# Reordering the first attention layer's start and the denominator and statistics work of a four-layer transformer kernel

## The chip, the cores and the metric

The kernel runs on one core of a Trainium2 chip. A core has five engines with an instruction queue each: TensorE (PE in the profile, matrix multiplication), VectorE (DVE), ScalarE (ACT), GpSimd (POOL) and SyncE (SP), which here only issues DMA transfers. A queue is worked through in order: an instruction that waits holds back all that stands behind it on its engine. Matmuls accumulate in PSUM, a memory of eight banks per partition; everything else lies in SBUF, 128 partitions wide.

The metric is the device time of one execution, in microseconds (us), as the median of several runs.

## The reference

Four residual layers are applied to x of shape 2048 rows by 576 columns (S = 2048, D = 576), in bfloat16: attention, MLP, attention, MLP, with the same two sets of weights used twice.

```python
def _A_ref(x, wqkv, wo):                       # H = 32 heads of 18
    q, k, v = split_heads(x @ wqkv)
    phi = lambda t: where(t > 0, t + 1, exp(t)) + 1e-6
    pq, pk = phi(q), phi(k)
    kv = einsum("bhsd,bhse->bhde", pk, v)      # sums over all rows
    z = einsum("bhsd->bhd", pk)
    num = einsum("bhqd,bhde->bhqe", pq, kv)
    den = einsum("bhqd,bhd->bhq", pq, z)[..., None] + 1e-6
    return merge_heads(num / den) @ wo

def _B_ref(x, w1, b1, w2, b2):                 # F = 4608
    return gelu(layernorm(x) @ w1 + b1) @ w2 + b2

x = x + _A_ref(layernorm(x), A_wqkv, A_wo)
x = x + _B_ref(layernorm(x), B_w1, B_b1, B_w2, B_b2)
x = x + _A_ref(layernorm(x), A_wqkv, A_wo)
x = x + _B_ref(layernorm(x), B_w1, B_b1, B_w2, B_b2)
```

Attention is linear: `kv` and `z` are sums over the whole sequence, so queries can be finished only after all keys and values have been seen.

## The kernel before

**Units.** Rows go in 16 tiles of 128 (t = 0 to 15); four tiles make a block of 512 rows (c = 0 to 3, j the tile within it). The 576 columns are five groups of heads, g = 0 to 3 with 126 columns (seven heads) and g = 4 with 72 (four heads). The four layers are li = 0 to 3, here called layer 1 to layer 4; layers 1 and 3 are attention (`layer_A`), 2 and 4 the MLP (`LayerB`).

**Layer norm pipe** (`LNPipe`). A row tile that is fed to it moves one stage with every tick: statistics on VectorE (two halves, L293 and L294, aggregate L299, variance plus epsilon `ln_u` in L302 or L304), then GpSimd computes `ln_rstd` (L309) and `ln_nmr` (L313), then the normalized tile goes to one of three `y_ring` buffers (on GpSimd L324, on VectorE L328), then five 128x128 transposes on TensorE write `tp` (L346) and ScalarE copies them to `yT` (L348). In the argument `after` the caller names an instruction behind which the statistics must stand in VectorE's queue; this sets an order only and is no wait.

**Attention, first loop.** For each tile: `k_proj` makes the keys in two halves of 288 columns, five matmuls each (L441), into one of four rotating PSUM banks (`ps_h`). phi is then built in one of two ways. `phi_from_psum`: exp on ScalarE (L381), a second ScalarE pass adding the constant (Identity, L382), then on VectorE a minimum with 1 (L383) and a maximum of the two (L385). `phi_by_dve`: exp on ScalarE (L368), the minimum on VectorE (L369), and one VectorE operation that reads PSUM directly (L371). Before the change the second half goes by `phi_by_dve` in layer 3 only. The buffers for the exponentials (`phi_e`) are three, those for the Identity results two. Then `pre_a1` ticks the pipe (in layer 1 it first feeds tile t + 3, whose statistics stand behind the last phi product), `v_proj` makes the values in two column halves of 252 and 324 (L454, L457), both in the single PSUM tile `v_ps` of two banks; ScalarE copies 504 columns (L459), and the last 72 go by ScalarE for t < 2 (L462) and by VectorE otherwise (L464). `kv_acc` adds the tile before into `kvacc` (L472), and from some t on one query projection `q_proj` is added per tile (L478).

In layer 1, `k_proj(1)` comes directly behind `k_proj(0)`. Tiles 0 and 1 are normalized on VectorE, the others on GpSimd.

**Attention, between the loops.** VectorE masks `kvacc` to the heads' diagonal blocks (`kvT`) and builds `zsel`. `kv_wo(g)` multiplies a group of `kvT` with `wo` and copies the result to `kvwo` (L528 on VectorE for odd g, L530 on ScalarE for even). `den_stage(c)` computes the denominators of block c (L538, L542), their reciprocal (L546, VectorE, one buffer) and `quad_rden` (L548, VectorE), a masked copy that lies ready as a matmul operand. `scale_stage(g, c)` broadcasts it to all columns of a group by one matmul (L554 into `rden_ps`), copies that on ScalarE (L556) and multiplies it into the queries `pq` on VectorE (L557).

**Attention, wo loop.** For each tile, `wo_stage` makes ten matmuls (L565), two halves with g = 0 to 4 in order, so the fifth needs the scaled queries of g = 4, into `wo_ps`, which alternates between two PSUM tiles (accA, accB): tile t's matmuls must wait for the residual sum of tile t - 2 (`residual`, L419, VectorE). The new row tile is stored, and tiles 0 to 3 are fed to the layer norm pipe for the next layer. Behind `wo_stage` come scales of the next block (two, two, one and none for j = 0 to 3), in layer 1 the query projections that are left, `den_stage(c + 2)` once per block, and one tick of the pipe.

**What sets the order.** TensorE's instructions are chained by hand in program order (`pe`), and start-up transfers likewise (`chained`). On the other engines the build orders instructions by estimated readiness, bound by data and by the orders named by hand (`add_manual_dep` with NOSYNC).

Of the kernel before, what the change touches and what calls it, by code (L numbers as in the profile page):

```python
# [8 lines left out]
ALU = mybir.AluOpType  # L9
# [25 lines left out]
def build(tc, A_x, A_wqkv, A_wo, B_w1, B_b1, B_w2, B_b2, out, dbg=None, n_layers=4):  # L35
    nc = tc.nc
    dbg = dbg or {}
    with ExitStack() as ctx:
# [225 lines left out]
        class LNPipe:  # L264
# [3 lines left out]
            def feed(self, xt, t, kind, norm_eng, evac_eng="dve", load_from=None, after=None):  # L268
                self.items.append(dict(stage=(0 if load_from is None else -1), xt=xt, t=t, kind=kind,
                                       norm=norm_eng, evac=evac_eng, load=load_from,  # L270
                                       after=after))
# [4 lines left out]
            def tick(self, transposes=1):  # L276
                land()
                for it in list(self.items):
                    st = it["stage"]
                    if st == 4 and it["evac"] != "dma":  # L280
                        if transposes == 0:
                            continue
                        transposes -= 1
                    if st == -1:
# [5 lines left out]
                    elif st == 0:  # L290
# [4 lines left out]
                        if it["after"] is not None:  # L295
                            for stats in (first, second):
                                tc.add_manual_dep(stats.ins, it["after"], NOSYNC, reason="statistics give way")
# [3 lines left out]
                        if it["kind"] == "A":  # L301
                            nc.vector.tensor_scalar(out=u[:], in0=mv[:, 1:2], scalar1=EPS, scalar2=None, op0=ALU.add)  # L302
                        else:
                            nc.vector.tensor_scalar(out=u[:], in0=mv[:, 1:2], scalar1=1.0 + EPS, scalar2=EPS * EPS,  # L304
                                                    op0=ALU.mult, op1=ALU.add)
                        it["mv"], it["u"] = mv, u
                    elif st == 1:
# [50 lines left out]

        lnp = LNPipe()
# [15 lines left out]
        def phi_from_psum(ps_ap, out_ap, rows, n, turned_cols=False):  # L375
# [6 lines left out]
            nc.scalar.activation(out=a_out, in_=ps_ap, func=ACT.Identity, bias=C1, scale=1.0)  # L382
# [46 lines left out]
        def layer_A(li, next_kind, pre_a1=None):  # L429
# [5 lines left out]
            def k_proj(t):  # L435
                tok = slice(t * P, (t + 1) * P)
                pk = blk.tile([P, D], BF16, name="pk", tag="blk")
                for half in range(2):
# [5 lines left out]
                    phi = phi_by_dve if li > 0 and half == 1 else phi_from_psum  # L444
# [3 lines left out]
            def v_proj(t):  # L448
# [4 lines left out]
                for k in range(KD):  # L453
                    pe(nc.tensor.matmul(vp[:, 0, 0:252], lhsT=yT[:, k, tok], rhs=wqkv_sb[:, k, 2 * D: 2 * D + 252],  # L454
                                     start=(k == 0), stop=(k == KD - 1)))
                for k in range(KD):
                    pe(nc.tensor.matmul(vp[:, 1, 0:324], lhsT=yT[:, k, tok], rhs=wqkv_sb[:, k, 2 * D + 252: 3 * D],  # L457
                                     start=(k == 0), stop=(k == KD - 1)))
                nc.scalar.copy(out=va[:, 0:4, 0:126].rearrange("p (b g) c -> p b g c", b=2),  # L459
                               in_=vp[:, :, 0:252].rearrange("p b (g c) -> p b g c", g=2))  # L460
                if t < 2:
# [24 lines left out]
            for t in range(NT):  # L486
                if t != 1 or li > 0:
                    k_proj(t)
                if t == 0 and li == 0:
                    k_proj(1)  # L490
# [41 lines left out]
            quad_rden = {}  # L532

            def den_stage(c):
# [10 lines left out]
                with nc.allow_low_precision("reciprocal of the denominator in the reference's bfloat16"):  # L545
                    nc.vector.reciprocal(out=rden[:], in_=dp[:, 0:P])  # L546
                quad = blk.tile([P, D], BF16, name="quad_rden", tag="blk")
                nc.vector.tensor_tensor(out=quad[:, 0:CA].rearrange("p (j n) -> p j n", j=4), in0=quad_mask[:],  # L548
                                        in1=rden[:].unsqueeze(1).to_broadcast([P, 4, P]), op=ALU.mult)
# [10 lines left out]
            def wo_stage(t):  # L560
# [8 lines left out]
                if xn is not None and next_kind == "B" and t < TPC:  # L569
                    lnp.feed(xn, t, "B", "pool", "act")  # L570
# [7 lines left out]
            den_stage(0)  # L578
            q_proj(*q_left.pop(0))
            kv_wo(1)  # L580
            den_stage(1)
# [3 lines left out]
            q_proj(*q_left.pop(0))  # L585
            for g in range(3, G):
                scale_stage(g, 0)
            kv_wo(3)
            kv_wo(4)
            q_proj(*q_left.pop(0))  # L590
            for t in range(NT):
# [3 lines left out]
                wo_stage(t)  # L595
                if c + 1 < NCA:
# [153 lines left out]
        def pre_a1_layer0(t):  # L750
            if t + 3 < NT:
                feed0(t + 3, after=dve_last["phi"])
# [79 lines left out]
```

## Time and profile before

| | |
|---|---|
| median of 3 runs | 778.01 us (777.93 to 779.69) |
| profiled execution, its own time | 778.13 us |
| its span, first to last instruction | 776.4 us |
| granted TensorE clock, mean | 1.000 |

Busy time of the engines in stretches of that execution (us):

| stretch | from, to | PE | DVE | ACT | POOL |
|---|---|---|---|---|---|
| layer 1, start | 0 to 18 | 13.64 | 11.34 | 8.70 | 6.44 |
| layer 1, rest of first loop, preparation | 18 to 84 | 65.32 | 49.00 | 54.07 | 32.01 |
| layer 1, half of the wo loop | 84 to 103 | 18.49 | 17.63 | 11.01 | 10.03 |
| rest of it, layer 2 | 103 to 397 | 294.00 | 90.66 | 104.25 | 35.06 |
| layer 3 up to the wo loop | 397 to 465 | 67.31 | 40.36 | 47.87 | 0.55 |
| rest | 482 to 777 | 290.83 | 51.10 | 101.06 | 26.67 |

How such lines are read: a timeline row gives the start in us from the beginning of the span, the length in us, the engine, the line of the kernel, the operation, the tile written and the tiles read, their sizes and the number of equal instructions in a row. In brackets stands how long the engine had been idle before it, and whose end it waited for. PE is TensorE and the length of a run of matmuls includes the pipeline's last result, so the next row can start before the one above has ended; the same holds for the other engines by smaller amounts. The step of an operation is therefore taken from one start to the next.

### The profile page before, as it was taken

The page shows a single profiled execution, that of the slowest core. Times are in us where ns is not written, and L with a number is a line of the kernel's source. Part 1 is how long each engine was busy: PE and PEld are TensorE (multiplying, and loading weights), DVE is VectorE, ACT ScalarE, POOL GpSimd, SP SyncE. Part 2 cuts the span into 40 slices and gives each one's busy share as a digit, 9 for nine tenths or more (in the row PEclk, how much of TensorE's full clock was granted, in tenths as well). Part 3 has the DMA queues.
Part 4 walks back from the last instruction along what each step waited for, and adds up shares of the span by engine and source line. Part 5 has one row for each costly group of instructions (what it writes and reads, how often), then busy time and mean ns, then how long its engine had stood idle before and what let it go on. Part 6 is the DMA issues. An engine that isn't in the chain of part 4 may idle for free.

```text
span 776.4 us, 15770 instructions
## 1 busy us (share of the span) xinstructions
PE 765.1 (99%) x6613; PEld 495.6 (64%) x6613; DVE 276.4 (36%) x711; ACT 335.4 (43%) x738; POOL 119.2 (15%) x185
## 2 busy tenths in 40 slices
PE   7999999999999999999999999999999999999998
PEld 4777664575477457646777766547745764675476
DVE  5786965045113603400355579520140032000000
ACT  4887746403620660164046675561065026304600
POOL 3573312012000301200100004210030011002000
PEclk9999999999999999999999999999999999999999
DMA  8990374106401720230440006730141033011000
GB/s 268 278 296 22 111 242 121 36 31 171 109 16 48 187 61 32 80 75 2 153 100 9 1 2 208 250 81 8 31 128 53 17 124 80 8 32 54 1 11 21
DMA packets 73761, 69.10 MB, mean 89 GB/s; under 512 B 34266, under 2 KB 58330, under 8 KB 73690
## 3 DMA queue, kind: packets, MB, share of 16 engines
q1 hardware_dynamic: 73690, 68.10, 30.2%
q8 instruction: 51, 0.84, 0.5%
q14 instruction: 20, 0.16, 0.1%
HBM read 45.67 MB, written 22.41 MB: 88 GB/s over the span
## 4 chain that ended last, share of the span: by engine, by line
PE 94%; DVE 3%; ACT 1%; issue 1%; POOL 0%; DVEq 0%; ACTq 0%; POOLq 0%
PE m_ps L716 36%; PE h_ps L666 20%; PE hp_ps L666 16%; PE k_ps L441 5%; PE q_ps L478 5%; PE wo_ps L565 4%; PE v_ps L457 3%; PE v_ps L454 2%; PE kvacc L472 1%; PE tp L346 1%; PE warm_ps L176 1%; PE rden_ps L554 1%; ACT rden_bc L556 1%; DVE pq L557 0%; DVE xn L419 0%
## 5 line engine op out<-in xcount | busy, mean ns | idle before, releaser
L716 PE MATMUL m_ps<-w_sb,hT 128*128 128x288 bf16 x2304 | 283.6, 286 | 0.0
L716 PEld LDWEIGHTS <-hT 128*128 128x128 bf16 x2304 | 224.8, 98 | 59.8 <-issue 3.4
L666 PEld LDWEIGHTS <-w_sb 64*128 64x128 bf16 x2304 | 124.6, 94 | 136.4 <-issue 1.9
L666 PE MATMUL hp_ps<-yT,w_sb 64*128 64x512 bf16 x1152 | 178.0, 376 | 0.0
L666 PE MATMUL h_ps<-yT,w_sb 64*128 64x512 bf16 x1152 | 148.0, 376 | 0.0
L671 ACT COPY relay_sb<-relay_sb 128x1 f32<-128x1 f32 x144 | 28.5, 198 | 264.7 <-PE h_ps L666 222.2
L309 POOL TENSOR_TENSOR ln_rstd<-ln_u,neg_half 128x1 f32<-128x1 f32 x64 | 36.4, 571 | 483.3 <-DVE ln_u L302 253.0
L662 ACT ACTIVATE hT<-h_ps,b1T 128x512 bf16<-128x512 f32 x144 | 91.0, 683 | 44.4 <-PE h_ps L666 44.4
L662 ACT ACTIVATE hT<-hp_ps,b1T 128x512 bf16<-128x512 f32 x144 | 91.1, 692 | 0.0
L419 DVE TENSOR_TENSOR xbf<-m_ps,xo 128x576 bf16<-128x576 f32 (+1 forms) x17 | 12.2, 721 | 221.4 <-PE m_ps L716 221.4
L419 DVE TENSOR_TENSOR xo<-m_ps,xo 128x576 f32<-128x576 f32 x16 | 12.1, 757 | 180.1 <-PE m_ps L716 180.1
L403 POOL TENSOR_TENSOR xo<-xo,b_bc 128x576 f32<-128x576 f32 x32 | 40.9, 1281 | 101.9 <-DMA xo<-x_d 61.5
L666 PE MATMUL h_ps<-yT,w_tail 64*128 64x512 bf16 x144 | 54.2, 376 | 0.0
L666 PE MATMUL hp_ps<-yT,w_tail 64*128 64x512 bf16 x144 | 54.1, 376 | 0.0
L478 PE MATMUL q_ps<-yT,wqkv_sb 128*126 128x512 bf16 (+1 forms) x200 | 50.0, 382 | 0.0
L565 PE MATMUL wo_ps<-kvwo,pq 126*128 126x288 bf16 (+1 forms) x320 | 43.5, 285 | 2.6 <-DVE xo L419 1.5
L441 PE MATMUL k_ps<-wqkv_sb,yT 128*128 128x288 bf16 x320 | 44.3, 286 | 0.0
L565 PEld LDWEIGHTS <-pq 126*128 126x128 bf16 (+1 forms) x320 | 30.4, 97 | 13.7 <-issue 3.5
L441 PEld LDWEIGHTS <-yT 128*128 128x128 bf16 x320 | 31.0, 98 | 11.4
L666 PEld LDWEIGHTS <-w_tail 64*128 64x128 bf16 x288 | 27.1, 94 | 17.1
L383 DVE TENSOR_SCALAR phi_e<-phi_e 128x288 bf16<-128x288 bf16 (+2 forms) x88 | 26.1, 297 | 25.0 <-ACT phi_e L381 24.9
L381 ACT ACTIVATE phi_e<-k_ps 128x288 bf16<-128x288 f32 x48 | 20.2, 420 | 34.2 <-PE k_ps L441 34.1
(98 smaller groups left out, 631.6 us busy)
## 6 DMA issues: line engine op xcount, KB each, us to landing
xo<-x_d SPq DMA_DIRECT2D x48, 288.0 KB, 3.9
x_d<-xo SPq DMA_DIRECT2D x32, 288.0 KB, 2.3
xl<-x_d SPq DMA_DIRECT2D x24, 288.0 KB, 4.3
y_d<-turned SPq DMA_DIRECT2D x40, 144.0 KB, 3.2
w_sb<-in_B_w_dram SPq DMA_DIRECT2D x6, 864.0 KB, 10.2
yT<-y_d SPq DMA_DIRECT2D x10, 512.0 KB, 4.1
w_sb<-in_B_w_dram SPq DMA_DIRECT2D x9, 512.0 KB, 5.4
x_d<-xn SPq DMA_DIRECT2D x16, 288.0 KB, 2.1
```

The costliest lines, as they stand in the source:

```text
L309: nc.gpsimd.tensor_tensor(out=rstd[:], in0=it["u"][:], in1=neg_half[:], op=ALU.pow)
L383: nc.vector.tensor_scalar(out=e[0:rows, 0:n], in0=e[0:rows, 0:n], scalar1=1.0, scalar2=1e-6, op0=ALU.min, op1=ALU.add)
L403: nc.gpsimd.tensor_tensor(out=xo[:], in0=xo[:], in1=b2_bc[:], op=ALU.add)
L419: total = nc.vector.tensor_tensor(out=xn[:, cols].rearrange("p (h n) -> p h n", h=nh), in0=ps, in1=xo[:, cols].rearrange("p (h n) -> p h n ...
L441: pe(nc.tensor.matmul(kp[:, 0:HALF], lhsT=yT[:, k, tok], rhs=wqkv_sb[:, k, D + half * HALF: D + (half + 1) * HALF], start=(k == 0), stop=( ...
L457: pe(nc.tensor.matmul(vp[:, 1, 0:324], lhsT=yT[:, k, tok], rhs=wqkv_sb[:, k, 2 * D + 252: 3 * D], start=(k == 0), stop=(k == KD - 1)))
L478: pe(nc.tensor.matmul(qp[0:GR[g], :], lhsT=wqkv_sb[:, k, GO[g]:GO[g] + GR[g]], rhs=yT[:, k, c * CA:(c + 1) * CA], start=(k == 0), stop=(k ...
L565: pe(nc.tensor.matmul(wp[:, half, 0:HALF], lhsT=pq[(g, c)][0:GR[g], j * P:(j + 1) * P], rhs=kvwo[g][0:GR[g], half * HALF:(half + 1) * HALF ...
L662: act_last["gelu"] = nc.scalar.activation(out=to, in_=ps, func=ACT.Gelu_apprx_tanh, bias=b1T[:, f:f + 1], scale=1.0).ins.name
L666: mm = pe(nc.tensor.matmul(dst[n], lhsT=wt, rhs=mv, start=(seen[n] == 0), stop=(seen[n] == 8)))
L671: relay = nc.scalar.copy(out=relay_sb[:, 1:2], in_=relay_sb[:, 0:1])
L716: pe(nc.tensor.matmul(acc[:, half, 0:HALF], lhsT=hT[f][:, j * P:(j + 1) * P], rhs=w2_sb[:, f, half * HALF:(half + 1) * HALF], start=(f == ...
```

## The change

Six things are reordered or moved; no matmul is added or dropped.

1. In layer 1, the second key half of tiles 0 and 1 goes by `phi_by_dve`, as in layer 3.
2. In layer 1, tile 0's values are copied in three pieces on ScalarE: bank 0 (252 columns) early, ordered behind the key passes, then 252 of bank 1, then the last 72. For tile 1 of layer 1 and tiles 0 and 1 of layer 3 the 72-column copy moves from ScalarE to VectorE.
3. In layer 1, the statistics of tile 3 are ordered behind the phi products of tile 0 instead of the last ones, and those of tile 4 behind the `ln_u` of tile 3.
4. The denominators of blocks 0 and 1 come one behind the other, ahead of a query projection; `kv_wo(3)` comes ahead of the last two scales.
5. `quad_rden` is split from `den_stage`. For blocks 2 and 3 it is ordered behind the next tile's residual sum.
6. In the wo loop, the statistics of tiles 0 to 3 are ordered behind the newest sum (`after="sum"`) and start one tick later (`hold=1`); their normalization and transposes come later by as much.

```diff
-            def feed(self, xt, t, kind, norm_eng, evac_eng="dve", load_from=None, after=None):
+            def feed(self, xt, t, kind, norm_eng, evac_eng="dve", load_from=None, after=None, hold=0):
...
+                    if it["hold"] > 0:
+                        it["hold"] -= 1
+                        continue
...
-                        if it["after"] is not None:
+                        after = dve_last["sum"] if it["after"] == "sum" else it["after"]
+                        if after is not None:
                             for stats in (first, second):
-                                tc.add_manual_dep(stats.ins, it["after"], NOSYNC, reason="statistics give way")
+                                tc.add_manual_dep(stats.ins, after, NOSYNC, reason="statistics give way")
...
+                        dve_last["u"] = var_eps.ins.name
...
-                    phi = phi_by_dve if li > 0 and half == 1 else phi_from_psum
+                    phi = phi_by_dve if half == 1 and (li > 0 or t < 2) else phi_from_psum
...
+                begin = li == 0 and t == 0
+                if begin:
+                    early = nc.scalar.copy(out=va[:, 0:2, 0:126], in_=vp[:, 0, 0:252].rearrange("p (g c) -> p g c", g=2))
+                    for keys in ("exp", "phi"):
+                        tc.add_manual_dep(early.ins, act_last[keys], NOSYNC, reason="keys before values")
                 for k in range(KD):
                     pe(nc.tensor.matmul(vp[:, 1, 0:324], lhsT=yT[:, k, tok], rhs=wqkv_sb[:, k, 2 * D + 252: 3 * D],
                                      start=(k == 0), stop=(k == KD - 1)))
-                nc.scalar.copy(out=va[:, 0:4, 0:126].rearrange("p (b g) c -> p b g c", b=2),
-                               in_=vp[:, :, 0:252].rearrange("p b (g c) -> p b g c", g=2))
-                if t < 2:
+                if begin:
+                    nc.scalar.copy(out=va[:, 2:4, 0:126], in_=vp[:, 1, 0:252].rearrange("p (g c) -> p g c", g=2))
+                else:
+                    nc.scalar.copy(out=va[:, 0:4, 0:126].rearrange("p (b g) c -> p b g c", b=2),
+                                   in_=vp[:, :, 0:252].rearrange("p b (g c) -> p b g c", g=2))
+                if begin:
                     nc.scalar.copy(out=va[:, 4, 0:72], in_=vp[:, 1, 252:324])
                 else:
                     nc.vector.tensor_copy(out=va[:, 4, 0:72], in_=vp[:, 1, 252:324])
...
                 if t == 0 and li == 0:
+                    phi0["dve"] = dve_last["phi"]
                     k_proj(1)
...
+                rden_of[c] = rden
+
+            def quad_stage(c, after=None):
                 quad = blk.tile([P, D], BF16, name="quad_rden", tag="blk")
-                nc.vector.tensor_tensor(out=quad[:, 0:CA].rearrange("p (j n) -> p j n", j=4), in0=quad_mask[:],
-                                        in1=rden[:].unsqueeze(1).to_broadcast([P, 4, P]), op=ALU.mult)
+                spread_out = nc.vector.tensor_tensor(
+                    out=quad[:, 0:CA].rearrange("p (j n) -> p j n", j=4), in0=quad_mask[:],
+                    in1=rden_of.pop(c)[:].unsqueeze(1).to_broadcast([P, 4, P]), op=ALU.mult)
+                if after is not None:
+                    tc.add_manual_dep(spread_out.ins, after, NOSYNC, reason="sums first")
...
                 if xn is not None and next_kind == "B" and t < TPC:
-                    lnp.feed(xn, t, "B", "pool", "act")
+                    lnp.feed(xn, t, "B", "pool", "act", after="sum", hold=1)
...
             den_stage(0)
+            quad_stage(0)
+            den_stage(1)
+            quad_stage(1)
             q_proj(*q_left.pop(0))
             kv_wo(1)
-            den_stage(1)
             for g in range(3):
                 scale_stage(g, 0)
             kv_wo(2)
             q_proj(*q_left.pop(0))
+            kv_wo(3)
             for g in range(3, G):
                 scale_stage(g, 0)
-            kv_wo(3)
             kv_wo(4)
...
                 wo_stage(t)
+                for late in list(rden_of):
+                    quad_stage(late, after=dve_last["sum"])
...
-                feed0(t + 3, after=dve_last["phi"])
+                feed0(t + 3, after=phi0["dve"] if t == 0 else dve_last["u"] if t == 1 else dve_last["phi"])
```

14 lines of the change are left out of this document (9 added, 5 removed).

## The prediction

> **What bounds the kernel now.** I read the page's first part, then what each engine waited for (only TensorE's rows matter when it is nearly always busy), and then the timelines around each of those waits. Columns of the waits: for whom and for what, microseconds in total, times, longest.
>
> ```profile
> span 776.4 us, 15770 instructions
> ...
> PE 765.1 (99%) x6613; PEld 495.6 (64%) x6613; DVE 276.4 (36%) x711; ACT 335.4 (43%) x738; POOL 119.2 (15%) x185
> ```
>
> ```profile
> PE tp L346 <- POOL y_ring L324: 2.8, 2, 2.5
> PE wo_ps L565 <- DVE xo L419: 1.5, 1, 1.5
> ...
> PE wo_ps L565 <- DVE kvwo L528: 0.9, 2, 0.5
> ...
> PE rden_ps L554 <- DVE quad_rden L548: 0.4, 2, 0.2
> ```
>
> TensorE is busy 765.1 of 776.4 us and its number of matmuls does not change, so only its holes can be won or lost. These rows and the 0.51 before v(1), in the row at 12.31 below, hold 6.1 us. The change reaches for all of them; the largest are two single holes, 2.5 us at the start and 1.5 us in layer 3.
>
> **The start: new key path, early value copy, statistics of row tile 3 brought forward.** TensorE's timeline (start, length, instruction, then the idle time in brackets):
>
> ```profile
> 7.68 2.61 PE L441 MATMUL k_ps<-wqkv_sb,yT 128*128 128x288 bf16 x20
> ...
> 10.67 0.85 PE L457 MATMUL v_ps<-wqkv_sb,yT 128*128 128x324 bf16 x5
> ...
> 12.31 0.70 PE L454 MATMUL v_ps<-wqkv_sb,yT 128*128 128x252 bf16 x5 [0.51 <-ACT v_ring L462]
> ...
> 13.79 1.39 PE L441 MATMUL k_ps<-wqkv_sb,yT 128*128 128x288 bf16 x10
> 17.72 0.45 PE L346 MATMUL tp<-ident,y_ring 128*128 128x128 bf16 x5 [2.54 <-POOL y_ring L324]
> ```
>
> The same stretch on ScalarE and VectorE, and the loads of the x rows (three issued together at 4.42; then the least, median and greatest time to landing of all x loads):
>
> ```profile
> 9.41 0.41 ACT L382 ACTIVATE phi_a<-k_ps 128x288 bf16<-128x288 f32 x1
> 9.72 0.41 ACT L381 ACTIVATE phi_e<-k_ps 128x288 bf16<-128x288 f32 x1
> 11.56 0.58 ACT L459 CAST v_ring<-v_ps 128x504 bf16<-128x504 f32 x1 [1.43 <-PE v_ps L457]
> 12.03 0.23 ACT L462 CAST v_ring<-v_ps 128x72 bf16<-128x72 f32 x1
> ```
>
> ```profile
> 10.32 0.51 DVE L385 TENSOR_TENSOR pk<-phi_a,phi_e 128x288 bf16<-128x288 bf16 x2
> ...
> 14.07 0.45 DVE L293 BATCH_NORM_STATS2 ln_st<-x 128x6 f32<-128x288 bf16 x1
> ...
> 15.59 0.13 DVE L302 TENSOR_SCALAR ln_u<-ln_mv 128x1 f32<-128x1 f32 x1
> ```
>
> ```profile
> 4.42 1.53 SPq L150 DMA_DIRECT2D x<-in_A_x_dram  x3
> ```
>
> ```profile
> DMA to landing us min/median/max: 2.2/4.1/5.7
> ```
>
> The hole of 2.54 us ends when tile 3 is normalized. Its statistics start at 14.07, behind the last key product; they could have started earlier, since the load was issued by 4.42 + 0.51 and even the slowest took 5.7, so the tile is there by 10.6. In the changed program the statistics stand behind the products of k(0) and one step of k(1).
>
> New times, all estimates from these rows. The key halves leave TensorE every 0.65 (2.61 / 4), so the exp of k(1)'s first half stays at 9.72. The exp of its second half writes a phi_e buffer (three exist) which the first product of the 10.32 row frees at about 10.63, so it runs from 10.68. The early copy is ordered behind it: one ScalarE step (9.41 to 9.72) is 0.31, so 10.99; 252 columns lie between 72 (0.23) and 504 (0.58), I take 0.38, done at 11.37. Here is a wait that before does not have: in the changed program the second half of the v(0) matmuls waits for that early copy, as both halves are one PSUM tile. That half starts at about 11.42 instead of 10.67, 0.75 late. From there to v(1) it was 1.64 (10.67 to 12.31), with a 504-column step of 0.47 (11.56 to 12.03) in it; a 252-column step is about 0.27, so 1.44, and v(1) is at 12.86. From v(1) to the end of k(2) the matmuls take 1.48 (12.31 to 13.79) plus ten of k at 0.122 ((2.61 - 1.39) / 10), together 2.70: TensorE asks for tile 3 at 15.57. Is it ready? Exp ends 11.09, one short VectorE step of 0.2, statistics at 11.3; first half to ln_u took 1.52 (14.07 to 15.59, with another tile's half inside, which the direct key product now replaces); ln_u to transposes 2.13 (15.59 to 17.72, on GpSimd). That is 14.95, so TensorE no longer waits, and the transposes begin at 15.57 instead of 17.72: **-2.15 us**. Bounds: -2.7 if the early copy held nothing up (k(2) ends at 13.79 + 1.22 = 15.01), and -1.3 if GpSimd and VectorE are each 0.7 later than worked out (14.95 + 1.4 = 16.4). I take -2.15, as each step has its row.
>
> The dropped Identity passes and the added copies are ScalarE work; ScalarE has a hole of 1.43 at 11.56 that hides them, except as told. The direct product of k(1)'s second half costs VectorE more than L385, but nobody on TensorE needs it until its kv matmuls, behind k(2).
>
> **Layer 3's beginning.** The 72-column copy of t = 0 and 1 goes from ScalarE to VectorE, behind the direct key product. Group row and timelines:
>
> ```profile
> L464 DVE CAST v_ring<-v_ps 128x72 bf16<-128x72 f32 x28 | 6.4, 229 | 8.5 <-ACT v_ring L459 8.2 <-issue 0.3
> ```
>
> ```profile
> 399.43 0.46 DVE L371 SCALAR_TENSOR_TENSOR pk<-k_ps,phi_e 128x288 bf16<-128x288 f32 x1
> ```
>
> ```profile
> 399.80 0.70 PE L454 MATMUL v_ps<-wqkv_sb,yT 128*128 128x252 bf16 x5
> ```
>
> v(2) reuses the one v_ps and started without waiting at 399.80. Its buffer now comes free at 399.43 + 0.40 + 0.23 = 400.06, plus a semaphore step: **+0.3 us** (0 if VectorE reaches the copy ahead of the product).
>
> **Denominators 1 and 2 together; kv_wo(3) ahead of the last scales.** The stretch before wo(0) is VectorE's back-to-back work; it ends with the same kvwo copy for which TensorE waits 0.9 in two layers. Nothing of that work goes; the third broadcast matmul now waits for a den bank to be freed by the second reciprocal. I take +0.1 to +0.15 a layer, kept within the two sums below, from -0.2 (the rden row's waits vanish) to +0.3.
>
> **Layer 1's wo loop: quad behind the sum, statistics one tick later.** First VectorE, then TensorE:
>
> ```profile
> 91.53 0.95 DVE L546 RECIPROCAL rden<-den_ps 128x128 bf16<-128x128 f32 x1
> ```
>
> ```profile
> 93.17 0.60 PE L554 MATMUL rden_ps<-quad_rden,head_bc 128*128 128x512 bf16 x2
> 93.61 0.44 PE L346 MATMUL tp<-ident,y_ring 128*128 128x128 bf16 x5
> 94.20 1.39 PE L565 MATMUL wo_ps<-kvwo,pq 126*128 126x288 bf16 x10
> ...
> 102.30 0.90 PE L565 MATMUL wo_ps<-kvwo,pq 126*128 126x288 bf16 x6
> ```
>
> The steps of VectorE, start to start, are read from layer 3 here:
>
> ```profile
> 468.82 0.95 DVE L546 RECIPROCAL rden<-den_ps 128x128 bf16<-128x128 f32 x1
> 469.69 0.40 DVE L293 BATCH_NORM_STATS2 ln_st<-xo 128x6 f32<-128x288 f32 x1
> 470.00 0.86 DVE L548 TENSOR_TENSOR quad_rden<-quad_mask,rden 128x512 bf16<-128x512 bf16 x1
> 470.79 0.45 DVE L294 BATCH_NORM_STATS2 ln_st<-xo 128x6 f32<-128x288 f32 x1
> 471.16 0.73 DVE L419 TENSOR_TENSOR xo<-wo_ps,xo 128x576 f32<-128x576 f32 x1
> 471.82 0.19 DVE L299 BATCH_NORM_AGGREGATE ln_mv<-ln_st 128x2 f32<-128x12 f32 x1
> 471.94 0.36 DVE L557 TENSOR_TENSOR pq<-pq,rden_bc 72x512 bf16<-72x512 bf16 x1
> ...
> 479.59 0.45 DVE L557 TENSOR_TENSOR pq<-pq,rden_bc 72x512 bf16<-72x512 bf16 x1
> ```
>
> Reciprocal 0.87, a statistics half 0.37, sum 0.66, aggregate 0.12. In the changed layer 1 the reciprocal (at about 91.45) is followed by two halves, sum(3), aggregate and only then the quad: 91.45 + 0.87 + 0.74 + 0.66 + 0.12 = 93.84, done at 94.24. The first broadcast of the next block thus moves from 93.17 to 94.3, 1.13 later. Of this, waits that before has further on are swallowed: 0.3 for wo(5) (94.20 against 93.61 + 0.28 of transposes: 0.44 less the 0.17 by which a row of ten k matmuls is longer than its steps), 0.3 for the last transposes (the second of the 2.8 row's two waits) and 0.2 for this quad. Net **+0.3 us** at wo(9), 102.30 before; bounds -0.4 (only the old waits go) and +1.1 (none is swallowed).
>
> **Layer 3's wo loop.** Here stood the 1.52 hole:
>
> ```profile
> 471.95 1.39 PE L565 MATMUL wo_ps<-kvwo,pq 126*128 126x288 bf16 x10 [1.52 <-DVE xo L419]
> ...
> 481.56 1.39 PE L565 MATMUL wo_ps<-kvwo,pq 126*128 126x288 bf16 x10
> ```
>
> With tile 0's statistics out of its way the reciprocal starts at about 468.62 (it cannot come sooner: sum(1) now waits for its matmuls). Sum(2) follows at 468.62 + 0.87 + 0.74 = 470.23, 0.93 before its old 471.16, so wo(4) opens at 471.0. But its fifth weight block needs the 72-row scale, and before that come sum, aggregate, quad (0.32, like a scale, 0.36 long at 471.94), ln_u (an estimate of 0.07, half an aggregate) and a half: 471.76, done 472.12. So wo(4) ends only 0.3 sooner. Then what was put off must be done in a full queue. From sum(2) to the 72-row scale of the next block VectorE has six sums (3.96), a reciprocal (0.87), two quads (0.64), four aggregates and ln_u (0.76), six halves (2.19) and five scales (1.66): 10.1 us, so that scale starts at about 480.3 instead of 479.59 and ends at 480.7. The last six matmuls of wo(8), which need it, take 0.74; two broadcasts (93.17 to 93.61) and the last transposes, which stood ahead of wo(8) and now stand behind, 0.72 more: wo(9) at 482.17 against 481.56, **+0.6 us**. Bounds: -1.5 (the hole goes and nothing replaces it) and +1.3 (a row's statistics of 0.93 and a slow quad more).
>
> ```profile
> 469.78 0.82 POOL L324 TENSOR_SCALAR y_ring<-xo,ln_rstd,ln_nmr 128x576 bf16<-128x576 f32 x1
> ```
>
> The quad at 470.00 took 0.86 while this normalization ran on GpSimd. The Trainium skill (SBUF — State Buffer, "SBUF: two separate sides") says VectorE operations with two SBUF inputs and a GpSimd operation that reads SBUF lock each other out of a shared port for a whole instruction, and this pair of rows agrees. By that rule the quad of block 3, now near 479.2, would meet tile 3's later normalization and the sum would be about 0.45 worse; by the rows' steps alone it is as above.
>
> **The sum.** -2.15 + 0.3 + 0.3 + 0.6 = -0.95. The profiled execution took 778.13 (its span of 776.4 and 1.7 around it), the median of the runs is 778.01. So 777.2 in the profiled run's terms and **777.0 us** against the median.
>
> **The rivals.** A) The late work costs nothing: VectorE catches up in the wo loops and layer 3's hole simply goes. Then -2.15 - 1.5 + 0.3 = -3.35, 774.7. For it: that hole is one named wait for one sum, and the sum comes 0.93 sooner. Against it: this row (engine busy time in that window, of 17.00):
>
> ```profile
> 465.00:482.00 17.00, 15.48 (x165) 10.79 (x164) 16.31 (x40) 8.47 (x15) 8.45 (x16) 1.00 0.57 174
> ```
>
> VectorE, the third number of the five, is busy 16.31, so there is nowhere to catch up.
>
> B) Slower: the put-off statistics make VectorE the bound of both wo loops. A tile's statistics cost 0.93 (0.74 + 0.19); each time the queue stands idle early for want of them, that time is missing later, and every sum and scale behind comes later by as much. At the full price of four tiles in two loops it is 7.4; from 0.93 a loop on (half of 2.15 - 0.3) the start's gain is gone. At three tiles a loop 5.6 - 1.85 = +3.7, 781.7; at two, 779.9. Against it: sum(2) and the reciprocal use most of the freed time at once.
>
> C) The change does not do what it says at the start: the early copy or the statistics stand behind something else, v(1) stays late, and tile 3 with it. Then -0.4 or so there, with +1.2 elsewhere: 778.8. Against it: every step above has a row.
>
> **How the numbers follow.** Forecast 46% (775.3 to 778.3 by the bounds of its terms), A 30%, B 14%, C 10%. Some 0.3% (2.3 us) is what a measurement of this kernel can tell from no change, so faster means below 775.7 and slower above 780.3. Faster: A and 6 of the forecast's 46, 36%. Slower: 10 of B's 14. Same: the remaining 54%. The range 774.2 to 779.3 takes in A and C and leaves out most of B.
>
> **What would show it.** Right: the wait of tp for y_ring falls from 2.8 to under 0.6 and transposes of tile 3 start near 15.6; a new wait of about 0.7 of the second v matmuls (v_ps) for ScalarE's v_ring copy near 11.4; v(2) of layer 3 waiting 0.3 for VectorE; rden_ps waiting about 1 us for quad in layer 1; wo_ps waiting for a 72-row pq instead of xo in layer 3. Wrong: no wait on v_ps at 11.4, or TensorE without holes in layer 3's wo loop (A), or sums and scales that hold TensorE for more than 2 us in a loop (B).

## The result and the profile after

The changed kernel takes 777.34 us (median of 18 runs, 777.01 to 778.14) against 778.56 for the kernel before on the same chip (18 runs, 777.74 to 779.97): a ratio of 0.9983 with a 95% interval of 0.9976 to 0.9990. It is faster, by 1.2 us, and that lies within the 0.3% that the prediction called no change. 777.0 was forecast. Only the two kernels with the old start (the one before and, further on, the run of the rest alone) have executions some 1.5 us longer, at a granted clock of 0.997 or 0.998 instead of 0.999 to 1.000, 26 of 71 and 7 of 11 in the rounds of the experiments; against the shorter executions of before alone (10 of the 18 here, median 778.06) the changed kernel gains 0.7 us.

The profiled execution took 777.09, with a span of 775.4. First, what TensorE waited for in the changed kernel (for whom and for what, us in total, times, longest):

```profile
PE warm_ps L176 <- DVE y_ring L171: 1.3, 1, 1.3
PE rden_ps L578 <- DVE ln_u L309: 0.9, 1, 0.9
PE rden_ps L578 <- DVE rden L564: 0.8, 2, 0.4
PE wo_ps L589 <- DVE pq L581: 0.7, 2, 0.5
PE rden_ps L578 <- DVE quad_rden L569: 0.6, 2, 0.3
PE v_ps L470 <- ACT v_ring L466: 0.6, 1, 0.6
PE wo_ps L589 <- DVE kvwo L545: 0.6, 2, 0.3
PE tp L352 <- POOL y_ring L330: 0.4, 1, 0.4
PE wo_ps L589 <- DVE xo L427: 0.4, 1, 0.4
PE v_ps L462 <- ACT v_ring L478: 0.3, 1, 0.3
```

The two big holes are gone, and the rest are smaller: none is over 0.9. Without the warm-up row they add up to 5.3 us, where the five rows of before added up to 6.1. Lines are those of the changed file: L578 is the broadcast that was L554, L589 the wo matmuls (L565), L470 and L462 the two value halves (L457, L454), L352 the transposes (L346). The 0.9 put down to `ln_u` belongs to the quad one instruction ahead of it: the trace names what ended nearest to the release.

TensorE's timeline of the changed kernel at the start, then at wo(0), wo(5) and wo(9) of layer 1, v(2) of layer 3, and wo(0), wo(4), wo(8) and wo(9) of layer 3:

```profile
7.29 2.61 PE L449 MATMUL k_ps<-wqkv_sb,yT 128*128 128x288 bf16 x20
...
11.06 0.85 PE L470 MATMUL v_ps<-wqkv_sb,yT 128*128 128x324 bf16 x5 [0.61 <-ACT v_ring L466]
...
12.48 0.70 PE L462 MATMUL v_ps<-wqkv_sb,yT 128*128 128x252 bf16 x5 [0.30 <-ACT v_ring L478]
...
15.19 0.44 PE L352 MATMUL tp<-ident,y_ring 128*128 128x128 bf16 x5
...
80.59 1.58 PE L589 MATMUL wo_ps<-kvwo,pq 126*128 126x288 bf16 x10 [0.29 <-DVE kvwo L545]
...
91.76 0.61 PE L578 MATMUL rden_ps<-quad_rden,head_bc 128*128 128x512 bf16 x2 [0.85 <-DVE ln_u L309]
...
100.30 1.40 PE L589 MATMUL wo_ps<-kvwo,pq 126*128 126x288 bf16 x10
...
398.09 0.70 PE L462 MATMUL v_ps<-wqkv_sb,yT 128*128 128x252 bf16 x5
...
458.06 0.38 PE L578 MATMUL rden_ps<-quad_rden,head_bc 128*128 128x512 bf16 x1 [0.38 <-DVE rden L564]
...
462.06 1.58 PE L589 MATMUL wo_ps<-kvwo,pq 126*128 126x288 bf16 x10 [0.29 <-DVE kvwo L545]
...
469.36 0.65 PE L589 MATMUL wo_ps<-kvwo,pq 126*128 126x288 bf16 x4 [0.37 <-DVE xo L427]
470.52 0.91 PE L589 MATMUL wo_ps<-kvwo,pq 72*128 72x288 bf16 x6 [0.51 <-DVE pq L581]
...
479.02 0.91 PE L589 MATMUL wo_ps<-kvwo,pq 72*128 72x288 bf16 x6 [0.18 <-DVE pq L581]
...
480.49 1.40 PE L589 MATMUL wo_ps<-kvwo,pq 126*128 126x288 bf16 x10
```

Two rows of before that the prediction did not need, wo(0) of both attention layers:

```profile
82.84 1.58 PE L565 MATMUL wo_ps<-kvwo,pq 126*128 126x288 bf16 x10 [0.46 <-DVE kvwo L528]
...
463.50 1.58 PE L565 MATMUL wo_ps<-kvwo,pq 126*128 126x288 bf16 x10 [0.47 <-DVE kvwo L528]
```

Since TensorE does the same matmuls in nearly the same order, the same matmul can be found in both traces, and the difference of its start says what was gained up to there. The first key matmul started at 7.68 in the one execution and at 7.29 in the other, before anything that the change touches; that 0.39 is taken off.

| matmul | before | changed | gain since k | this stretch | forecast |
|---|---|---|---|---|---|
| tp of tile 3 | 17.72 | 15.19 | 2.14 | +2.14 | +2.15 |
| wo(0), layer 1 | 82.84 | 80.59 | 1.86 | -0.28 | -0.1 to -0.15 |
| wo(9), layer 1 | 102.30 | 100.30 | 1.61 | -0.25 | -0.3 with the row above |
| v(2), layer 3 | 399.80 | 398.09 | 1.32 | -0.29 | -0.3 |
| wo(0), layer 3 | 463.50 | 462.06 | 1.05 | -0.27 | -0.1 to -0.15 |
| wo(9), layer 3 | 481.56 | 480.49 | 0.68 | -0.37 | -0.6 with the row above |

So 2.1 us were won in the first 16 us, and two thirds of it were given back in five stretches. In each of them a row names what TensorE waits for; for v(2) of layer 3 it is VectorE's small copy, shown with the account of the prediction.

### The profile page after: what moved, and what is told of

It reads as the page before. It is cut to its first block, busy times and chain, and to the rows that moved or that the text cites. A ratio compares the mean times of both kernels' runs of the same rounds, so it can differ in the third digit from the quotient of the medians.

```text
span 775.4 us, 15774 instructions
## 1 busy us (share of the span) xinstructions
PE 765.1 (99%) x6613; PEld 495.0 (64%) x6613; DVE 277.7 (36%) x714; ACT 335.1 (43%) x734; POOL 120.5 (16%) x185
## 4 chain that ended last, share of the span: by engine, by line
PE 94%; DVE 4%; issue 1%; ACT 1%; DMA 0%; POOL 0%; DVEq 0%; ACTq 0%
PE m_ps L744 37%; PE h_ps L694 20%; PE hp_ps L694 16%; PE q_ps L494 5%; PE k_ps L449 5%; PE wo_ps L589 4%; PE v_ps L470 3%; PE v_ps L462 2%; PE kvacc L488 1%; PE tp L352 1%; PE rden_ps L578 1%; PE warm_ps L176 1%; DVE rden L564 1%; DVE xo L427 0%; DMA x_d<-xo 0%
## 5 line engine op out<-in xcount | busy, mean ns | idle before, releaser
L589 PE MATMUL wo_ps<-kvwo,pq 126*128 126x288 bf16 (+1 forms) x320 | 43.9, 285 | 1.7 <-DVE pq L581 0.7
L589 PEld LDWEIGHTS <-pq 126*128 126x128 bf16 (+1 forms) x320 | 30.2, 97 | 13.1 <-DVE pq L581 1.8
```

The lines of the kernel that those rows point to most:

```text
L589: pe(nc.tensor.matmul(wp[:, half, 0:HALF], lhsT=pq[(g, c)][0:GR[g], j * P:(j + 1) * P], rhs=kvwo[g][0:GR[g], half * HALF:(half + 1) * HALF ...
```

## The experiments

Each kernel was timed in five rounds against the kernel before on the same chip. The intervals of single edits overlap, and the ratios hold the longer executions of before, so each run is read together with the table's matmuls in its own trace, counted from its own first key matmul (k), as this table does for all of them (us; the changed kernel: tile 3's transposes 7.90 after k, wo(0) of layer 3 454.77, wo(9) 473.20; before: 10.04, 455.82, 473.88).

| run | median | ratio to before (95%) | tp(3) | wo(0), layer 3 | wo(9), layer 3 |
|---|---|---|---|---|---|
| start only | 776.28 | 0.9973 (0.9962 to 0.9984) | 8.32 | 454.38 | 472.43 |
| rest only | 780.61 | 1.0019 (1.0011 to 1.0028) | 10.03 | 456.64 | 475.05 |
| no early copy | 778.14 | 0.9995 (0.9986 to 1.0004) | 8.95 | 455.76 | 474.17 |
| statistics at once | 776.72 | 0.9978 (0.9969 to 0.9987) | 7.89 | 454.77 | 472.63 |
| own bank | 776.79 | 0.9976 (0.9967 to 0.9984) | 7.71 | 454.51 | 472.91 |
| no early copy, ordered | 776.69 | 0.9977 (0.9968 to 0.9987) | 7.44 | 454.33 | 472.73 |
| quad at once | 777.67 | 0.9987 (0.9979 to 0.9996) | 7.90 | 455.18 | 473.59 |
| old preparation | 776.21 | 0.9974 (0.9964 to 0.9983) | 7.89 | 454.16 | 472.24 |
| small copies back | 777.00 | 0.9981 (0.9972 to 0.9990) | 8.14 | 454.65 | 473.07 |
| all three, new loops | 775.99 | 0.9964 (0.9950 to 0.9978) | 7.71 | 453.80 | 471.89 |
| all three, old loops | 775.38 | 0.9959 (0.9946 to 0.9972) | 7.39 | 453.18 | 471.25 |
| all three, quad late in layer 3 alone | 774.97 | 0.9954 (0.9941 to 0.9967) | 7.37 | 453.16 | 470.85 |

### The start alone, the rest alone

The first run puts preparation, quads and statistics back, the second puts the start and the small copies back. The edit of the first, cut (`kv_wo(3)` also goes behind the last two scales again):

```diff
-            den_stage(1)
-            quad_stage(1)
             q_proj(*q_left.pop(0))
             kv_wo(1)
+            den_stage(1)
+            quad_stage(1)
...
-                for late in list(rden_of):
-                    quad_stage(late, after=dve_last["sum"])
...
                     den_stage(c + 2)
+                    quad_stage(c + 2)
...
-                    lnp.feed(xn, t, "B", "pool", "act", after="sum", hold=1)
+                    lnp.feed(xn, t, "B", "pool", "act")
```

> The changed kernel with its preparation, quads and wo-loop statistics put back as they were before; only layer 1's start and the place of the 72-column copies are changed. Theory (the places add up: start -2.15, layer 3's beginning +0.3, and each attention layer's preparation and wo loop gives back some 0.5): 1.8 us faster than the kernel before, about 0.9 faster than the changed kernel; layer 3's hole before wo(4) stands again at about 1.5. Rival (the wo loops' new order is part of the gain): not faster than the changed kernel, under 1.2 us against before.

> Only the preparation, the quads and the wo-loop statistics in the new order; layer 1's start and the small copies as before. Theory: slower than before by about 0.9 us (two preparations of 0.15 to 0.3, layer 1's loop +0.25, layer 3's loop +0.4), with the 2.5 us hole of tile 3 at the start. Rival: faster than before by up to 1.5, since the hole before wo(4) of layer 3 goes.

By the medians the start alone is 2.1 us faster than before and 1.06 faster than the whole change; by its matmuls it is 1.45 ahead of before at wo(9) of layer 3. The rest alone is slower than before, 0.19% or 1.5 us by the ratio and 1.17 at wo(9). The parts add up: -1.45 and +1.17 make -0.28, and the whole change's -0.68 differs by 0.40, about as much as tile 3 came later in the trace of the start alone (8.32 against 7.90). The rival, that the new order of the loops is where the gain is from, falls: the rest does remove layer 3's hole (its row of `wo_ps` for `xo` is down from 1.5 to 0.4) and still loses. Within the start, the new key path and the earlier statistics were not taken apart: which of the two brings how much of the 2.1 us no run shows. Two rows of the start alone, from its waits:

```profile
PE wo_ps L589 <- DVE xo L427: 1.5, 1, 1.5
...
PE v_ps L470 <- ACT v_ring L466: 1.0, 1, 1.0
```

The first is layer 3's hole, back as expected. The second shows the early copy's wait at 1.0 instead of 0.6; the section on the hardware returns to it.

### The early copy

In the changed kernel the second half of v(0) waits 0.61 us, until ScalarE has copied the first bank. The first attempt took the early copy out:

```diff
-                    early = nc.scalar.copy(out=va[:, 0:2, 0:126], in_=vp[:, 0, 0:252].rearrange("p (g c) -> p g c", g=2))
...
+                whole = nc.scalar.copy(out=va[:, 0:4, 0:126].rearrange("p (b g) c -> p b g c", b=2),
+                                       in_=vp[:, :, 0:252].rearrange("p b (g c) -> p b g c", g=2))
```

> The changed kernel without the early copy: tile 0's values are copied in one piece of 504 columns and one of 72 on ScalarE, behind the keys. Theory (the second half of the v(0) matmuls waits for the early copy, as it is the same PSUM tile): no wait there, v(1) about 0.55 us sooner, transposes of tile 3 at about 14.6 instead of 15.2, and 0.5 us faster than the changed kernel. Rival (the copy by bank is what lets v(1) start early): 0.3 us slower, v(1) waiting longer.

A miss: 0.8 slower than the changed kernel. Its ScalarE timeline says why, and it is not the copy:

```profile
11.49 0.69 ACT L354 COPY yT<-tp 128x640 bf16<-128x640 bf16 x1 [1.43 <-PE tp L352]
12.08 0.42 ACT L375 ACTIVATE phi_e<-k_ps 128x288 bf16<-128x288 f32 x1
12.38 0.59 ACT L468 CAST v_ring<-v_ps 128x504 bf16<-128x504 f32 x1
```

With the early copy and its order gone, the build moved the copy of tile 2's rows ahead of the exp of k(1)'s second half. That copy waits for transposes until 11.49, and the exp, ready long before, stands behind it in the queue until 12.08 (10.34 in the changed kernel); the values and, by way of VectorE, tile 3's statistics come after it. TensorE waits 1.69 for v(1):

```profile
13.15 0.70 PE L462 MATMUL v_ps<-wqkv_sb,yT 128*128 128x252 bf16 x5 [1.69 <-ACT v_ring L474]
```

So this run removed two things at once. Two more separate them. One takes the early copy out and holds ScalarE's order (tile 2's rows behind the values); the other holds that order too, but keeps the early copy and gives the second half a PSUM tile of its own. Both edits are cut to their main lines:

```diff
+                            if t == 2 and "values" in phi0:
+                                tc.add_manual_dep(turned_in.ins, phi0.pop("values"), NOSYNC, reason="values before rows")
```

```diff
+                second = ps_h.tile([P, 512], F32, name="v2_ps", tag="h") if begin else vp[:, 1, :]
...
-                    pe(nc.tensor.matmul(vp[:, 1, 0:324], lhsT=yT[:, k, tok], rhs=wqkv_sb[:, k, 2 * D + 252: 3 * D],
+                    pe(nc.tensor.matmul(second[:, 0:324], lhsT=yT[:, k, tok], rhs=wqkv_sb[:, k, 2 * D + 252: 3 * D],
```

> The copy of tile 0's values in one piece of 504 columns and one of 72 again, but now ScalarE's copy of tile 2's rows is ordered behind them, so that the exp of k(1)'s second half stays where it is in the changed kernel. Theory (the loss of the run without the early copy came from ScalarE's order alone, in which the copy of tile 2's rows had gone ahead of the exp): v(1) at about 11.95 with k starting at 7.3, tile 3 at 14.65, 0.5 us faster than the changed kernel and 1.3 faster than the run without order. Rival (the early copy itself brings the gain): still 0.3 or more slower than the changed kernel.

> The changed kernel, but for tile 0 the second half of the values goes into a PSUM tile of its own (one of the four rotating banks), and ScalarE's order is held: early copy, second copy, 72 columns, then tile 2's rows. The computation is the same. Theory (the early copy is right, the one PSUM tile is what makes TensorE wait): no wait of the second half, which starts 0.55 to 0.6 sooner; v(1) waits only for the early copy; transposes of tile 3 wait for GpSimd at about 14.65 instead of starting at 15.2: 0.5 us faster than the changed kernel. Rival (tile 3's rows are ready no sooner than 15.2 whatever TensorE does): no difference.

By the medians they are 0.65 and 0.55 faster than the changed kernel. The matmuls bear out the first (tile 3 comes 0.46 sooner, wo(9) of layer 3 0.47) and the second by half (0.19 and 0.29, where 0.5 was expected). First the run without the early copy, then that with a bank of its own; k starts at 7.27 and 7.32:

```profile
10.26 0.85 PE L468 MATMUL v_ps<-wqkv_sb,yT 128*128 128x324 bf16 x5
...
11.90 0.70 PE L464 MATMUL v_ps<-wqkv_sb,yT 128*128 128x252 bf16 x5 [0.49 <-ACT v_ring L476]
...
14.71 0.45 PE L352 MATMUL tp<-ident,y_ring 128*128 128x128 bf16 x5
```

```profile
10.30 0.85 PE L473 MATMUL v_ps<-wqkv_sb,yT 128*128 128x324 bf16 x5
11.50 0.45 PE L352 MATMUL tp<-ident,y_ring 128*128 128x128 bf16 x5 [0.34 <-POOL y_ring L330]
...
15.03 0.45 PE L352 MATMUL tp<-ident,y_ring 128*128 128x128 bf16 x5 [0.37 <-POOL y_ring L330]
```

In both the second half no longer waits. The bank of its own then meets the next limit, GpSimd's normalized rows (0.34 and 0.37). The order in ScalarE's queue, keys and values before rows, is worth 1.5 us at tile 3 (8.95 without it, 7.44 with it, and nothing else differs); the copy by bank itself costs more than it brings, because both banks belong to one tile.

### Statistics at once, quads at once

> The changed kernel with the statistics of tiles 0 to 3 in the wo loops at once, as before; quads behind the sums and everything else as changed. Theory (putting them off leaves VectorE idle early and makes the 72-row scale late): 0.3 to 0.6 us faster than the changed kernel; layer 3's wo(8) no longer waits for the scale. Rival (the quad behind the sum is what costs): no difference, under 0.2 either way, or slower by up to 1 as sum(2) comes late again.

The edit is the last line pair of the section's first diff. 0.6 faster than the changed kernel; wo(0) of layer 3 stands where it stood, wo(9) comes 0.57 sooner. Its TensorE timeline at wo(4) and wo(8):

```profile
469.88 0.65 PE L589 MATMUL wo_ps<-kvwo,pq 126*128 126x288 bf16 x4 [0.89 <-DVE xo L427]
471.05 0.91 PE L589 MATMUL wo_ps<-kvwo,pq 72*128 72x288 bf16 x6 [0.51 <-DVE pq L581]
...
478.26 1.40 PE L589 MATMUL wo_ps<-kvwo,pq 126*128 126x288 bf16 x10
```

Counted from k, wo(4) is 0.5 later than in the changed kernel and wo(8) level with it (0.06 later), but wo(8) then has no wait for the 72-row scale and wo(9) comes 0.57 sooner: in layer 3, putting the statistics off buys half a microsecond early and repays it twice.

The counterpart keeps the statistics late and makes the quad at once (`quad_stage(c + 2)` directly behind `den_stage(c + 2)`):

> The changed kernel with quad_rden made at once behind the reciprocal, ahead of the next sum, as before; statistics still put off. Theory (the quad behind the sum makes the next block's first broadcast wait 0.85 us in layer 1): that wait goes, 0.2 to 0.5 us faster than the changed kernel, though sum(2) of layer 3 comes 0.3 to 0.8 later. Rival (the sums first are worth it): 0.3 to 0.8 slower.

Here the rival was right: 0.33 slower. In layer 1 the wait of 0.85 for the quad goes, as expected, but transposes then wait as long for GpSimd, which is fed by the late statistics:

```profile
98.21 0.53 PE L352 MATMUL tp<-ident,y_ring 128*128 128x128 bf16 x5 [0.85 <-POOL y_ring L330]
```

With the kernel before, these traces hold all four orders. The time from wo(0) to wo(9) of the same layer, in us:

| quads of blocks 2 and 3 | statistics | trace | layer 1 | layer 3 |
|---|---|---|---|---|
| at once | at once | before | 19.46 | 18.06 |
| late | at once | statistics at once | 19.72 | 17.86 |
| at once | late | quad at once | 20.12 | 18.41 |
| late | late | changed | 19.71 | 18.43 |

In layer 3 the late statistics cost 0.35 to 0.57 and the late quad gains 0.20 when the statistics are at once. In layer 1 the late quad costs 0.26 by itself, and the late statistics cost 0.66 only where the quad is not late as well. (Before also has the old preparation; two more traces with both at once, the start alone and the old loops below, agree with it to 0.01.)

### The preparation

> The changed kernel with the order between the loops as before: den_stage(1) behind kv_wo(1), kv_wo(3) behind the last scales. Theory (each preparation lost 0.28 us by the third broadcast's wait for the second reciprocal): 0.5 us faster than the changed kernel, the waits of rden_ps for rden gone, the kvwo wait back at 0.45 a layer. Rival (what the preparation loses TensorE would lose anyway to VectorE's queue): no difference.

The edit is the first part of the first diff, with `kv_wo(3)` put behind the last two scales again. It gained 1.1 us, twice what was expected. By its matmuls wo(0) comes 0.30 sooner in layer 1 and 0.30 more in layer 3, which is the theory; another 0.35 is from layer 3's wo loop, where VectorE's queue came out with one half of tile 0's statistics ahead of the reciprocal, in a gap, so that sum(2) was there in time for wo(4):

```profile
465.45 0.45 DVE L296 BATCH_NORM_STATS2 ln_st<-xo 128x6 f32<-128x288 f32 x1
465.82 0.74 DVE L581 TENSOR_TENSOR pq<-pq,rden_bc 126x512 bf16<-126x512 bf16 x2
466.48 0.95 DVE L564 RECIPROCAL rden<-den_ps 128x128 bf16<-128x128 f32 x1
```

### The small copies, and what beats both kernels

> The changed kernel with one edit: the 72-column copies of tiles 0 and 1 in layer 3 are on ScalarE again. Theory (on VectorE that copy stands behind the direct key product, and v(2) waits for it): v(2) of layer 3 starts right behind k(2), 0.29 us sooner against k's start, and the kernel is 0.3 us faster than the changed one. Rival (VectorE's queue there is free in time, the 0.29 comes from elsewhere): no difference.

In this kernel v(2) of layer 3 follows v(1) by 2.71 (395.94 to 398.65 in its TensorE timeline), in the changed one by 2.97 (395.12 to 398.09): 0.26 sooner, as expected, and the median is 0.34 lower.

The three single edits that helped (old preparation, no early copy with the order held, small copies back) were then put together, with three forms of the wo loops:

> What the runs so far call for, with the changed wo loops kept: preparation as before, no early copy but ScalarE's order held, layer 3's small copies on ScalarE. Theory (the gains of the single edits add: -1.1, -0.65, -0.3): 2.0 us faster than the changed kernel, 775.3. Rival (they overlap, as the later stages are bound by VectorE): 0.7 to 1.2 faster only.

> As the run before, with the wo loops (quads and statistics) as in the kernel before. Theory (with the old preparation the new loops are worth nothing on balance: the run of the start alone and the run with the old preparation stood at 776.28 and 776.21): the same as the run with the new loops within 0.3, near 775.3, with layer 3's hole of 1.5 back and layer 1's wait for the quad gone. Rival (the loops' gain of sums first shows once preparations are cheap): 0.5 or more slower.

> As the run with old loops, but in layer 3 alone the quads go behind the next sum; statistics at once. Theory (layer 1 is hurt by the late quad, layer 3 gets sum(2) 0.8 sooner): hole before wo(4) of layer 3 0.7 to 0.9 instead of 1.5, layer 1's loop as before, 0.5 faster than the run with old loops, 774.8. Rival (layer 3's VectorE queue gives it back before wo(9)): within 0.2 of the run with old loops.

```diff
-                for late in list(rden_of):
+                for late in list(rden_of) if li > 0 else []:
                     quad_stage(late, after=dve_last["sum"])
...
                     den_stage(c + 2)
+                    if li == 0:
+                        quad_stage(c + 2)
```

With the new loops 775.99, 1.35 faster than the changed kernel: between theory and rival. In its trace tile 3 starts 7.71 after k, where the single edit had 7.44. With the old loops 775.38, 0.6 faster, where the theory said the same within 0.3. By the traces half of that is no price of the loops: 0.32 of the 0.64 at wo(9) of layer 3 is there at tile 3 already, before any loop; layer 1's new loop costs 0.31, and layer 3's 0.02, so that there the theory holds. With the quad late in layer 3 alone 774.97, the fastest of all: 3.2 us or 0.46% (0.33 to 0.59) faster than before by the medians, 3.0 at wo(9). The last two kernels at wo(4) of layer 3:

```profile
469.02 1.39 PE L589 MATMUL wo_ps<-kvwo,pq 126*128 126x288 bf16 x10 [1.53 <-DVE xo L429]
```

```profile
468.06 0.65 PE L589 MATMUL wo_ps<-kvwo,pq 126*128 126x288 bf16 x4 [0.73 <-DVE xo L429]
469.22 0.91 PE L589 MATMUL wo_ps<-kvwo,pq 72*128 72x288 bf16 x6 [0.51 <-DVE pq L581]
```

The sum comes 0.8 sooner and the scale holds six of the ten matmuls 0.5 longer, so 0.3 is left there, and 0.40 at wo(9).

## Why the prediction came out

**The start** was right to the hundredth in its sum and in its main steps. The new wait of the second value half, which the order of instructions showed, was forecast to move it 3.74 after k (11.42 less 7.68) and it was 3.77; v(1) 5.18 and 5.19; tile 3's transposes 7.89 and 7.90, held by TensorE's own work and not by GpSimd. The first statistics of tile 3, and GpSimd's normalization of it, in the changed kernel:

```profile
11.07 0.45 DVE L296 BATCH_NORM_STATS2 ln_st<-x 128x6 f32<-128x288 bf16 x1
```

```profile
13.78 0.83 POOL L330 TENSOR_SCALAR y_ring<-x,ln_rstd,ln_nmr 128x576 bf16<-128x576 bf16 x1
```

They stood at 14.07 and 16.84 before; the rows of tile 3 are now ready at 14.61, 0.58 before TensorE takes them. The hundredth holds luck: three more traces with the same start give 7.89 or 7.90 for tile 3, but two, in which k itself begins later, give 8.14 (small copies back) and 8.32 (start alone). That the tile, and not the early reading, makes the wait was shown by the run with a bank of its own, which keeps the early reading and has no wait.

**Layer 3's beginning**, +0.3: measured +0.29, and undone by putting the small copies back. No row of the waits names it, but in the changed kernel v(2) starts at 398.09, right behind the end (398.04) of the small copy that it was to wait for:

```profile
397.81 0.23 DVE L480 CAST v_ring<-v_ps 128x72 bf16<-128x72 f32 x1
```

**The preparation** was mis-sized. Forecast at 0.1 to 0.15 a layer, it cost 0.28 and 0.27. The mechanism was named, a third broadcast waiting for the second reciprocal, but its wait alone is 0.38 in each layer, and only part of it is repaid by a shorter kvwo wait (0.46 to 0.29 in layer 1). The run with the old preparation gives both back.

**Layer 1's wo loop**: the first broadcast of the next block was to come 1.1 late and wait about 1; it waits 0.85, and by wo(9) 0.25 is left. That is the late quad's price: with the statistics at once it stays (19.72 in the table of the four orders). With the preparation it is 0.53 instead of 0.3.

**Layer 3's wo loop** went step by step as worked out: wo(4) waits for sum(2) for 0.37 only, then its fifth weights wait 0.51 for the 72-row scale; wo(8) does the same again for 0.18; from v(2) to wo(9), the preparation included, 0.64 is given back (0.6 forecast). The further 0.45 that the prediction worked out for the quad of block 3, should it meet a normalization on GpSimd, did not come: it took 0.58 beside one, but 0.57 in the kernel before too, which the prediction had not looked at, and block 2's quad came free of its own (0.37 instead of 0.86).

**The sum.** The terms were -0.95; the matmuls show -0.68, which fits the 0.7 against the shorter executions of before. The 0.27 between them is the size of the preparation's miss (0.55 for both layers instead of 0.2 to 0.3). The medians differ by 1.2, more than either, since the longer executions of before are gone with the new start; no term of the prediction stood for that. None of those executions was profiled, so why the old start has them stays open. That the median came out only 0.3 from the forecast is in part luck: the two misses have opposite signs.

**The rivals.** A (the loops cost nothing) falls with the run of the rest alone. B (the put-off statistics make VectorE the bound of both loops) has the mechanism right in layer 3 alone, where the loop loses 0.37 and the statistics at once bring 0.57 back; layer 1's 0.25 is the quad's. Both stay far below the 0.93 a loop from which B would have decided. C is excluded by the first rows of the trace.

## What to carry to other kernels

In a queue as full as VectorE's here, moving work later mostly chose which instruction waits, and the same move can pay in one loop and cost in another (the late quad won 0.20 in layer 3 and lost 0.26 in layer 1); before putting work off, look whether the queue would stand idle for want of it. In this build an early read of part of a PSUM tile held up the writes to all of it (0.61 us), so a copy by bank needs tiles by bank. And taking out one instruction can let the build reorder others: compare the orders before reading a result as that instruction's price.

## What the runs showed of the hardware

The wait for the early copy was 0.6 in the changed kernel and 1.0 in the trace of the start alone, though the start's instructions are the same. In the latter VectorE's short step of phi was stretched while GpSimd normalized tile 2; first VectorE, then GpSimd, both with the start alone:

```profile
9.69 0.24 DVE L376 TENSOR_SCALAR phi_e<-phi_e 128x288 bf16<-128x288 bf16 x1 [0.38 <-ACT phi_e L375]
10.30 0.68 DVE L391 TENSOR_SCALAR phi_e<-phi_e 128x288 bf16<-128x288 bf16 x1 [0.38 <-ACT phi_e L388]
```

```profile
10.07 0.82 POOL L330 TENSOR_SCALAR y_ring<-x,ln_rstd,ln_nmr 128x576 bf16<-128x576 bf16 x1
```

It took 0.68 instead of 0.24 and ended at 10.98, just behind GpSimd's 10.89. In the changed kernel the same step began ahead of GpSimd's (9.91) and was short:

```profile
9.78 0.23 DVE L391 TENSOR_SCALAR phi_e<-phi_e 128x288 bf16<-128x288 bf16 x1 [0.38 <-ACT phi_e L388]
```

Behind this step in VectorE's queue stands the product that frees a `phi_e` buffer; the exp of k(1)'s second half waits for that buffer, and the early copy stands behind the exp. Counted from k, GpSimd began 2.25 in with the start alone (10.07 less 7.82) and 2.62 in the changed kernel; that shift became 0.4 on TensorE. A third trace, with the small copies back, lies in line: GpSimd began 2.07 in, the step took 0.50 and the wait was 0.9.

It works the other way round too. In the changed kernel's layer 3 an operation of GpSimd on one element per partition took 1.13 for tile 1 and 0.27 for tile 0 (the third row is tile 2's `ln_rstd`, 1.36 where tile 0's took 0.55); GpSimd first, then VectorE:

```profile
470.57 0.27 POOL L319 TENSOR_SCALAR ln_nmr<-ln_mv,ln_rstd 128x1 f32<-128x1 f32 x1
...
472.73 1.13 POOL L319 TENSOR_SCALAR ln_nmr<-ln_mv,ln_rstd 128x1 f32<-128x1 f32 x1
...
475.04 1.36 POOL L315 TENSOR_TENSOR ln_rstd<-ln_u,neg_half 128x1 f32<-128x1 f32 x1
```

```profile
473.04 0.37 DVE L581 TENSOR_TENSOR pq<-pq,rden_bc 126x512 bf16<-126x512 bf16 x1
...
473.39 0.42 DVE L581 TENSOR_TENSOR pq<-pq,rden_bc 126x512 bf16<-126x512 bf16 x1
```

The 1.13 ends at 473.86, with the second of two scales that read two SBUF operands (473.81). The Trainium skill (SBUF — State Buffer, "SBUF: two separate sides") describes such blocking as a lock on a shared port, held for a whole instruction; these rows agree with it in where the operation ends, but it had begun 0.31 before the first of the two scales, which they leave unexplained. The prediction had priced the block at the quad; it showed in GpSimd's chain instead, and the transposes of tile 2 waited 0.4 for their rows there, which no step of the prediction had.
